# Single statistics passes between matmul groups, earlier residual sums, and one forward step ahead of an inverse step

## The chip, the cores and the metric

The kernel runs on one core of a Trainium2 chip. The metric is device time in microseconds (us); several executions give a median. A profile comes from one execution and shows each engine: TensorE (PE, its weight loads PEld), VectorE (DVE), ScalarE (ACT), GpSimd (POOL) and the queue that issues transfers (SP). Each engine works through its own list of instructions in order and waits on semaphores for the others.

## The reference

One sequence of 2048 tokens with 1024 features passes through four layers, A, B, A, B, with the same weights both times:

```
x = x + A(layernorm(x))      # A: 2-D real FFT over tokens and features, times a filter, inverse FFT
x = x + B(layernorm(x))      # B: mish(x @ w1 + b1) @ w2, w1 is 1024 x 3584, w2 is 3584 x 1024
```

and again. The layer norm subtracts the mean of a row of 1024 features and divides by the root of variance plus 1e-5. Mish is h * tanh(softplus(h)). Values are bf16, sums fp32.

## The kernel before, in words

The 2048 tokens are 16 tiles of 128, kept in SBUF as XS[0..15]. Every instruction is recorded in program order into a list for its engine, with the semaphore waits that its tiles ask for, so the order of calls in the source is the order on each engine.

**Layer A** does both transforms as matmuls in stages: a first stage (`s1`), then for each of eight groups g a forward step in two halves (`s2`, matmuls at L741, copied out at L776 by ScalarE or L778 by VectorE), a forward transform in two parts (`s3`, L786 to L789; ScalarE copies at L798, VectorE multiplies by the filter at L800 to L807), an inverse transform (`i1`, L842, copied by ScalarE at L858) and an inverse step (`i2`, L872 and L904). Results go to PSUM through pairs of banks taken in turn, four pairs in all. The order of these pieces is a string of numbers written out by hand in `order_A`; 221 stands for `s2` of group 2, half 1, and 400 for `i1` of group 0, part 0. In the first layer A the filter is also put together between steps (VectorE copies at L1043).

**Layer B** starts before the last stage of layer A is through. The first product with w1, `mm1`, takes 512 tokens (or a half of 256) and one group of 256 columns of w1: two runs of eight matmuls (L1220), each with its Mish on ScalarE (L1224), which frees the bank; three banks take turns. While the second halves of groups 1 to 3 run, ScalarE also makes the row sums of tiles 6 and 7 for their layer norm, in `stats_act`: one pass that copies and sums, one that squares and sums (L451, two per tile). VectorE turns the sums into mean and scale (L462 to L513), normalises (L522), and TensorE transposes the tiles (L1181, copied by VectorE at L1186) for the next `mm1`.

The larger part of layer B multiplies blocks by a scheme with seven products instead of eight. For w1 that is `quads`: in turn n of its loop the products (L1260) go to six banks, VectorE adds them up (L1265), and ScalarE applies Mish (L1270). Between the additions of two turns a hook, `after(n)`, puts in other work: statistics of tiles 8 to 11, their normalisation (`normal`), and the residual sums of tiles 12 to 15 (`residual`, L1498), which add layer A's result to XS. The last layer B has ten turns in this loop, the first has eight. In a turn the next product into a bank waits for the addition that reads that bank. After `quads` come the products with w2 (L1359, added at L1402 and L1410).

The lines that the change touches in `after(n)`, with `first` = 6 in the last layer and 4 in the first:

```
for j in {first + 1: (12, 13), first + 2: (14,), first + 3: (15,)}.get(n, ()):
    residual(j)
```

Of the kernel before, what the change touches and what calls it, by code (L numbers as in the profile page):

```python
# [5 lines left out]
ACT = mybir.ActivationFunctionType  # L6
# [174 lines left out]
class KB:  # L181
# [261 lines left out]
                writes=rr)  # L443
        self.op(self.dve, lambda e: e.reciprocal(r, a), writes=rr)

    def stats_act(self, j):
        act = self.act
        x, sums, rs, junk = self.XS[:, j, :], self.BN[:, j, 0:2], self.r_mv[j], self.junk
        rs.begin()
        for i, f in enumerate((ACT.Copy, ACT.Square)):  # L450
            self.op(act, lambda e, i=i, f=f: e.activation(junk.ap, x, f, accum_out=sums[:, i:i + 1]),  # L451
                    reads=[self.r_xs[j]], writes=[junk.res], parts=[rs])

# [551 lines left out]
    @staticmethod  # L1005
    def order_A():


        order = ("200 201 210 211 300 301 220 310 400 221 311 401 230 320 410 500 231 321 411 501 330 331 420 510 240 511 421 241 "
                 "250 251 340 341 520 350 430 260 521 431 440 261 351 441 530 531 360 361 270 450 451 271 540 541 550 551 460 370 "  # L1010
                 "461 371 560 561 470 471 570 571")
        return [tuple(map(int, w)) for w in order.split()]
# [144 lines left out]
    def layer_B(self, li, last):  # L1157
# [14 lines left out]
        def transposed(c, t, xn, eng=None, bank=None):  # L1172
            if bank is None:
                bank = 6 + nt[0] % 2
                nt[0] += 1
            xn.unread = False
            if t == 0:
                open_xt(c)
            fns = []
            for db in range(8):  # L1180
                fns.append(lambda e, db=db: e.transpose(PSb[:, bank, db * P:(db + 1) * P], xn.ap[:, db * P:(db + 1) * P],  # L1181
                                                        self.IDENT[:]))
            self.group(fns, reads=[xn.res, self.r_ident], writes=[self.r_bank[bank]])
            dst = XT[c].ap[:, :, t * P:(t + 1) * P]
            src = PSb[:, bank, :].rearrange("p (a b) -> p a b", b=P)
            fn = (lambda e: e.activation(dst, src, ACT.Copy)) if eng is act else (lambda e: e.tensor_copy(dst, src))  # L1186
            self.op(eng or dve, fn, reads=[self.r_bank[bank]], parts=[r_xt[c][t // 2]])
# [14 lines left out]
        def turn(n):  # L1202
            for _ in range(min(n, len(turning))):
                turning.pop(0)()

        def mm1(c, fg, half=None, mid=()):
            wb = self.w1_buf[fg]
            x = XT[c]
            tok = slice(0, 512) if half is None else slice(256 * half, 256 * half + 256)
            w = tok.stop - tok.start  # L1210
            for fl in range(2):
                if fl:
                    for f in mid:
                        f()
                ft = 2 * fg + fl
                bank = nh[0] % 3
                nh[0] += 1
                fns = []
                for db in range(8):
                    fns.append(lambda e, db=db, bank=bank, fl=fl: e.matmul(  # L1220
                        PS[:, bank, 0:w], wb.ap[:, db, fl * P:(fl + 1) * P], x.ap[:, db, tok], start=(db == 0), stop=(db == 7)))
                self.group(fns, reads=[wb.res] + (r_xt[c] if half is None else [r_xt[c][half]]), writes=[self.r_bank[bank]])
                at, ra = at_of(c, ft), r_at[c % 2][ft]
                self.op(act, lambda e, bank=bank, ft=ft, at=at: e.activation(at[:, tok], PS[:, bank, 0:w], ACT.Mish,  # L1224
                                                                      bias=self.B1[:, ft:ft + 1]),
                        reads=[self.r_bank[bank], self.r_b1], writes=[ra])
# [118 lines left out]
        def load_b(stages, n, k):  # L1345
            PB[n][k] = load_w2(stages[n][1], k, f"R{(2 * n + k + 1) % 4}")
# [20 lines left out]
        def products(p, s_off, stages, extra, loads=True):  # L1367
# [83 lines left out]
            for n, t in turn_of:  # L1451
                a, b, g, start = stages[n]
                bank = sets[g][t]
                if n or t:
                    tile_product(n, t, bank, ap[a], lambda k: part(a, k), start)
                after(b, t, bank)
                for f, k in sums.get((n, t), ()):
                    f(k)
                if t == 3 and n < 5 and loads:
                    for k in range(2):  # L1460
                        if stages is STD or (n, k) != (4, 0):
                            load_b(stages, n + 2, k)
                extra(n, t)
# [9 lines left out]
        def at_tiles(c):  # L1473
            r_at[c] = [None] * NF
            for k in range(2):
                off = self.ob["A"] + 14336 * (2 * k + c)
                AT[c][k] = b = self.alloc(f"AT{c}{k}", off, [NF // 2, 512])
                for i in range(NF // 2):
                    r = r_at[c][2 * i + k] = Res(f"AT{c}_{2 * i + k}")
                    r.inherit(b.res)  # L1480
                    self.live.append((off + i * 1024, off + i * 1024 + 1024, r))
# [15 lines left out]
        def residual(j):  # L1497
            self.op(dve, lambda e: e.tensor_tensor(self.XS[:, j, :], self.XS[:, j, :], YS[:, j - 4, :], ALU.add),  # L1498
                    reads=[r_ys[j // 4 - 1]], writes=[self.r_xs[j]])

        def turns(c, *ts):
            return [lambda t=t: transposed(c, t, xn[4 * c + t]) for t in ts]
# [50 lines left out]
            xn[j] = self.apply(j)  # L1553
        for fg in range(1, 4):
            mm1(0, fg, 1)
            if fg < 3:
                self.stats_act(5 + fg)
        if not last:
            mm1(0, 4)
        at_tiles(1)  # L1560
        B = {"B11": (XT[0].ap[:, 0:4, :], r_xt[0]), "B21": (XT[0].ap[:, 4:8, :], r_xt[0])}
        order = list(early)
        if last:
            block, corner, run = quads(list(range(4, 14)), order, B, [k * 1024 for k in (102, 140)])
            for n, bank in ((0, 3), (1, 4), (2, 5), (3, 0)):
                block(n, bank)
            corner(1, 4)
            turns(1, 0)[0]()
            corner(2, 5)
            turns(1, 1)[0]()  # L1570
            corner(3, 0)
        else:
            mm1(0, 5, mid=turns(1, 0, 1))
# [13 lines left out]
        def normal(j):  # L1587
            if j % 4 == 0:
                open_xt(j // 4)
            turned(j // 4, j % 4, self.apply(j))  # L1590
# [33 lines left out]
        def after(n):  # L1624
            again = {0: 7, 4: 8, 5: 9} if last else {0: 7}
            if n in again:
                self.fill_slot(order[again[n]], plain + again[n])
            if 1 <= n < 4:
                load_b(STD, n // 3, (n - 1) % 2)
            first = 6 if last else 4  # L1630
            if last:
                if n in (0, 2, 4, 5):
                    self.stats_act(8 + (0, 2, 4, 5).index(n))
                if n == 5:
                    self.xn_buf = self.xn_out + [self.alloc(f"XN{i}", self.ob["XN2"] + i * 2048, [self.D]) for i in range(2)]
                if n in (5, 7):
                    self.sums_to_mv(n + 3, 2)
                    self.scales(n + 3, 2)
            elif n < 4:
                self.stats_dve(8 + n)  # L1640
            elif n == 4:
                self.scales(8, 4)
            if n >= first:
                normal(8 + n - first)
                turn(4)
            for j in {first + 1: (12, 13), first + 2: (14,), first + 3: (15,)}.get(n, ()):
                residual(j)
        run(after, lead)
        self.junk = self.alloc("JUNK2", self.ob["JUNK2"], [self.D])
# [68 lines left out]
        order = [ws[n % 3] for n in range(14)]  # L1718
# [94 lines left out]
```

## Time and profile before

| | |
|---|---|
| median of 3 runs | 927.1 us (926.85 to 933.89) |
| profiled execution, span | 923.2 us |
| TensorE busy | 877.7 us, 95% |
| VectorE busy | 623.4 us, 68% |
| ScalarE busy | 435.0 us, 47% |
| GpSimd busy | 147.7 us, 16% |
| transfers | 175.98 MB, mean 191 GB/s |

The shares are means over stages. The page also gives the chain of work that ended last, followed back from the end, by engine and line. A list of waits gives, for each engine, which line waited for which line of another engine. A timeline gives start, duration, engine, line, operation and tiles; in brackets stands the idle time before an instruction and what ended it. Matmul ends are modelled, so a matmul's shown duration can run past the start of the next.

### The profile page before, as it was taken

Reading aid. Unit: us, or ns where it says so; the run is one execution under the profiler, and the core shown is the slowest. Engines: PE = TensorE matmul, PEld = TensorE weight load, DVE = VectorE, ACT = ScalarE, POOL = GpSimd, SP = SyncE. Lnnn points to the kernel's source line nnn. Section 1 sums busy time; section 2 is a strip of 40 time slices with the busy share of each in tenths; the row PEclk is TensorE's granted clock in tenths of the full one; section 3 lists DMA queues with packets and bytes.
Section 4 is the critical chain, followed back from the end, with each engine's and each line's share of the span. In section 5 each row is a group of like instructions: output and inputs, shape, how many; then the busy total and the mean of one; then the engine's idle time right before and its main releaser. Section 6 shows DMA issues by size and latency. Waiting matters only on the chain.

```text
span 923.2 us, 13610 instructions
## 1 busy us (share of the span) xinstructions
PE 877.7 (95%) x5503; PEld 471.1 (51%) x5503; DVE 623.4 (68%) x995; ACT 435.0 (47%) x645; POOL 147.7 (16%) x170
## 2 busy tenths in 40 slices
PE   0899889999999999999998998999999999999998
PEld 0677576444444444444456766754444444444443
DVE  7798468686889667568767765676747655554463
ACT  7898485456203485420018966757540025552000
POOL 0732004960004651010121200000000000000000
PEclk9999999999999999999999999999999999999999
DMA  9979861575786388364723786345166645732432
GB/s 279 284 249 287 219 194 67 210 266 139 262 281 239 131 317 298 121 233 143 281 92 114 221 217 161 137 175 184 23 197 189 204 148 180 269 121 86 173 129 102
DMA packets 153502, 175.98 MB, mean 191 GB/s; under 512 B 75000, under 2 KB 132568, under 8 KB 153320
## 3 DMA queue, kind: packets, MB, share of 16 engines
q1 hardware_dynamic: 140256, 130.32, 45.9%
q0 software_dynamic: 10032, 42.90, 12.5%
q10 hardware_dynamic: 3152, 1.90, 0.7%
q8 instruction: 43, 0.70, 0.3%
q14 instruction: 19, 0.16, 0.0%
HBM read 130.78 MB, written 40.89 MB: 186 GB/s over the span
## 4 chain that ended last, share of the span: by engine, by line
PE 88%; DVE 6%; ACT 3%; SPq 2%; DMA 1%; issue 0%; DVEq 0%
PE PS L1359 37%; PE PS L1260 30%; PE PS L1220 6%; PE PS L741 3%; PE PS L842 2%; PE PS L872 2%; SPq L251 2%; PE PS L1071 2%; PE PS L634 1%; PE PS L651 1%; ACT ARENA L640 1%; PE PS L1181 1%; PE PS L904 1%; PE PS L1060 1%; ACT ARENA L451 1%; PE PS L656 1%
## 5 line engine op out<-in xcount | busy, mean ns | idle before, releaser
L1359 PE MATMUL PS<-ARENA 128*128 128x512 bf16 x1568 | 340.1, 379 | 0.0
L1260 PE MATMUL PS<-ARENA 128*128 128x512 bf16 (+1 forms) x1288 | 280.4, 379 | 0.8 <-DVE ARENA L1265 0.8
L1359 PEld LDWEIGHTS PS<-ARENA 128*128 128x128 bf16 x1568 | 153.3, 98 | 184.5
L1265 DVE TENSOR_TENSOR ARENA<-PS,ARENA 128x512 f32<-128x512 f32 x230 | 157.1, 691 | 100.2 <-PE PS L1260 92.4
L1260 PEld LDWEIGHTS PS<-ARENA 128*128 128x128 bf16 x1288 | 125.3, 98 | 153.3 <-DVE ARENA L1265 3.6
L1270 ACT ACTIVATE ARENA<-ARENA,B 128x512 bf16<-128x512 f32 x138 | 98.8, 721 | 69.1 <-DVE ARENA L1265 63.8
L573 ACT ACTIVATE ARENA<-PS 128x512 f32<-128x512 f32 (+3 forms) x86 | 61.6, 726 | 110.6 <-PE PS L1260 92.5
L1153 POOL TENSOR_TENSOR ARENA<-ARENA 128x512 bf16<-128x512 bf16 x56 | 71.5, 1278 | 74.3 <-DVE ARENA L522 61.1
L451 ACT ACTIVATE ARENA<-XS 128x1024 bf16<-128x1024 bf16 x60 | 63.2, 1053 | 36.6 <-DVE XS L1410 33.0
L1220 PE MATMUL PS<-ARENA 128*128 128x256 bf16 (+1 forms) x528 | 73.4, 295 | 3.4 <-DVE ARENA L1186 1.9
L1384 DVE TENSOR_TENSOR ARENA<-ARENA 128x3584 bf16<-128x3584 bf16 x32 | 63.9, 2017 | 0.0
L1410 DVE TENSOR_TENSOR XS<-PS,ARENA 128x512 bf16<-128x512 f32 x52 | 35.7, 689 | 39.0 <-PE PS L1359 38.7
L1220 PEld LDWEIGHTS PS<-ARENA 128*128 128x128 bf16 x528 | 50.3, 98 | 22.3 <-DVE ARENA L1186 3.3
L1402 DVE TENSOR_TENSOR ARENA<-PS,ARENA 128x512 f32<-128x512 f32 x48 | 32.9, 688 | 28.0 <-PE PS L1359 27.6
L1224 ACT ACTIVATE ARENA<-PS,B 128x256 bf16<-128x256 f32 (+1 forms) x66 | 33.0, 515 | 29.0 <-PE PS L1220 28.8
L1270 ACT ACTIVATE ARENA<-PS,B 128x512 bf16<-128x512 f32 x46 | 31.5, 685 | 18.4 <-PE PS L1260 18.4
L1398 DVE TENSOR_TENSOR ARENA<-ARENA,XS 128x512 f32<-128x512 f32 x52 | 36.8, 731 | 0.5
L442 ACT ACTIVATE RS<-MV,EPS 128x1 f32<-128x1 f32 (+2 forms) x11 | 3.3, 296 | 71.5 <-DVE MV L564 70.1
L741 PE MATMUL PS<-FD,ARENA 128*128 128x256 bf16 (+1 forms) x256 | 31.4, 271 | 2.5 <-ACT ARENA L640 2.5
L842 PE MATMUL PS<-ARENA 128*128 128x256 bf16 x256 | 32.6, 273 | 1.0 <-DVE ARENA L807 0.6
L798 ACT ACTIVATE ARENA<-PS 128x1024 bf16<-128x1024 f32 x30 | 30.4, 1046 | 5.0 <-PE PS L789 5.0
L1235 DVE TENSOR_TENSOR ARENA<-ARENA 128x2048 f16<-128x2048 bf16 x16 | 25.3, 1583 | 9.0 <-PE PS L1220 8.7
(102 smaller groups left out, 811.4 us busy)
## 6 DMA issues: line engine op xcount, KB each, us to landing
ARENA<-in_B_w_dram SPq DMA_DIRECT2D x30, 896.0 KB, 6.7
ARENA<-w1s_scratch SPq DMA_DIRECT2D x28, 896.0 KB, 4.7
ARENA<-w2s_scratch SPq DMA_DIRECT2D x24, 896.0 KB, 6.6
w1s_scratch<-ARENA POOLq DMA_DIRECT2D x14, 896.0 KB, 4.6
ARENA<-in_B_w_dram SPq DMA_DIRECT2D x24, 512.0 KB, 4.3
u_scratch<-ARENA SPq DMA_DIRECT2D x14, 512.0 KB, 4.9
ARENA<-u_scratch SPq DMA_DIRECT2D x14, 512.0 KB, 6.0
w2s_scratch<-ARENA POOLq DMA_DIRECT2D x8, 896.0 KB, 4.1
```

What stands on the lines that cost most here:

```text
L451: self.op(act, lambda e, i=i, f=f: e.activation(junk.ap, x, f, accum_out=sums[:, i:i + 1]), reads=[self.r_xs[j]], writes=[junk.res], parts ...
L573: fn = (lambda e: e.activation(dst, src, ACT.Copy)) if scale is None else \
L741: fns.append(lambda e: e.matmul(dst, at(r), FD[:, t:t + n], start=start, stop=stop))
L842: fns.append(lambda e, c=c, part=part: e.matmul(ps[:, c * 256:(c + 1) * 256], yk.ap[:, part, c * P:(c + 1) * P], t[:, (128, 0)[part]:(384, ...
L1153: self.op(self.pool, lambda e, dst=A(dst), x=A(x), y=A(y), op=op: e.tensor_tensor(dst, x, y, op), reads=[b.res] + list(after), writes=[b.rs])
L1220: fns.append(lambda e, db=db, bank=bank, fl=fl: e.matmul(PS[:, bank, 0:w], wb.ap[:, db, fl * P:(fl + 1) * P], x.ap[:, db, tok], start=(db ...
L1260: self.group([lambda e, db=db: e.matmul(PS[:, bank, :], A[:, db, :], mov[:, db, :], start=(start and db == 0), stop=(db == 3), skip_group_ ...
L1265: self.op(dve, lambda e: e.tensor_tensor(dst.ap, PS[:, bank, :], x.ap, ALU.add), reads=[self.r_bank[bank], x.res], writes=[dst.res])
L1270: self.op(act, lambda e: e.activation(at, src, ACT.Mish, bias=self.B1[:, ft:ft + 1]), reads=[res, self.r_b1], writes=[ra])
L1359: self.group([lambda e, i=i, k=k, b=PB[n][k].ap: e.matmul(PS[:, bank, :], ap[:, i, t * P:(t + 1) * P], b[:, i - 7 * k, :], start=(start an ...
L1384: self.op(dve, lambda e: e.tensor_tensor(ap[dst][:, f, :], ap[x][:, f, :], ap[y][:, f, :], op), reads=part(x, k) + part(y, k), writes=part ...
L1398: self.op(dve, lambda e: e.tensor_tensor(a[t], a[t], x, ALU.add), reads=[rx], writes=[r[t]])
```

## The change

It has three parts, all of them moves; no arithmetic is added or removed.

1. `stats_act` can do one of its two passes. The four passes over tiles 6 and 7, which followed groups 1 and 2 in pairs, now follow groups 1, 2, 3 and one later piece of work one at a time. The later piece is group 4 in the first layer B and a corner product of `quads` in the last. The aim is that Mish of a group doesn't stand behind two passes.
2. In the last layer B's `quads` loop the residual sums of tiles 12 and 13 move from turn 7 to turns 1 and 3; those of 14 and 15 stay in turns 8 and 9. In the first layer B the turns stay what they were (5, 6, 7).
3. In `order_A` the second half of group 2's forward step (221) comes ahead of the first inverse transform (400), in both layers A.

```
-    def stats_act(self, j):
+    def stats_act(self, j, passes=(0, 1)):
...
-        rs.begin()
-        for i, f in enumerate((ACT.Copy, ACT.Square)):
+        if passes[0] == 0:
+            rs.begin()
+        for i in passes:
+            f = (ACT.Copy, ACT.Square)[i]
...
-        order = ("200 201 210 211 300 301 220 310 400 221 311 401 230 ...
+        order = ("200 201 210 211 300 301 220 310 221 400 311 401 230 ...
...
         for fg in range(1, 4):
             mm1(0, fg, 1)
-            if fg < 3:
-                self.stats_act(5 + fg)
+            self.stats_act(6 + fg // 3, ((fg - 1) % 2,))
         if not last:
             mm1(0, 4)
+            self.stats_act(7, (1,))
...
             corner(1, 4)
+            self.stats_act(7, (1,))
             turns(1, 0)[0]()
...
-            for j in {first + 1: (12, 13), first + 2: (14,), first + 3: (15,)}.get(n, ()):
+            late = {1: (12,), 3: (13,), 8: (14,), 9: (15,)} if last else {5: (12, 13), 6: (14,), 7: (15,)}
+            for j in late.get(n, ()):
                 residual(j)
```

More of the change, by code (lines that the diff above doesn't have):

```diff
@@ L1006, in order_A @@
     def order_A():
-        order = ("200 201 210 211 300 301 220 310 400 221 311 401 230 320 410 500 231 321 411 501 330 331 420 510 240 511 421 241 "
+        order = ("200 201 210 211 300 301 220 310 221 400 311 401 230 320 410 500 231 321 411 501 330 331 420 510 240 511 421 241 "
                  "250 251 340 341 520 350 430 260 521 431 440 261 351 441 530 531 360 361 270 450 451 271 540 541 550 551 460 370 "
```

## Prediction

> **What bounds the kernel now.** I read, in this order: the page's shares and the chain that ended last, TensorE's list of waits, the timelines of TensorE and ScalarE around each named wait, and the chain inside those stretches. The page first:
>
> ```profile
> PE 877.7 (95%) x5503; PEld 471.1 (51%) x5503; DVE 623.4 (68%) x995; ACT 435.0 (47%) x645; POOL 147.7 (16%) x170
> PE 88%; DVE 6%; ACT 3%; SPq 2%; DMA 1%; issue 0%; DVEq 0%
> ```
>
> TensorE carries 88% of the chain, at the full granted clock in all 40 slices. No edit removes a matmul. The change can only gain idle time of TensorE, so I list who makes it wait (total us, times, longest us):
>
> ```profile
> PE PS L1220 <- ACT ARENA L1224: 1.4, 3, 0.6
> PE PS L1260 <- DVE ARENA L1265: 0.8, 1, 0.8
> PE PS L786 <- DVE ARENA L778: 0.8, 1, 0.8
> PE PS L842 <- DVE ARENA L807: 0.6, 1, 0.6
> ```
>
> Four waits lie where the edits are: L1220 (first product of layer B behind Mish), L1260 behind L1265 (the quadrant loop behind a VectorE addition), and L786 and L842 in layer A. Now their places. First TensorE, then ScalarE, early in the first layer B (start, duration, instructions, idle before in brackets):
>
> ```profile
> 134.39 4.53 PE L1220 MATMUL PS<-ARENA 128*128 128x256 bf16 x40
> 139.53 2.77 PE L1220 MATMUL PS<-ARENA 128*128 128x256 bf16 x16 [0.62 <-ACT ARENA L1224]
> 142.47 3.63 PE L1220 MATMUL PS<-ARENA 128*128 128x512 bf16 x16 [0.17 <-ACT ARENA L1224]
> ```
> ```profile
> 136.79 1.06 ACT L451 ACTIVATE ARENA<-XS 128x1024 bf16<-128x1024 bf16 x1
> 137.97 1.06 ACT L451 ACTIVATE ARENA<-XS 128x1024 bf16<-128x1024 bf16 x1
> 139.02 0.82 ACT L1224 ACTIVATE ARENA<-PS,B 128x256 bf16<-128x256 f32 x2
> 139.74 1.05 ACT L451 ACTIVATE ARENA<-XS 128x1024 bf16<-128x1024 bf16 x1
> 141.97 1.40 ACT L1224 ACTIVATE ARENA<-PS,B 128x256 bf16<-128x256 f32 x3
> ```
>
> Both passes of tile 6 stand in ScalarE's queue ahead of group 2's Mish, which had its matmuls since 137; the product cycles through three banks, so TensorE stops at 139.53 until that Mish frees one. The same with tile 7 at 142.47.
>
> The quadrant loop of the second layer B, from its chain:
>
> ```profile
> 654.42 0.69 DVE ARENA L1265
> 657.08 0.54 DVE FD L522
> 657.62 1.20 DVE XS L1498 x2
> 658.82 0.61 DVE ARENA L1265
> 659.48 4.49 PE PS L1260 x20
> ```
>
> Between two additions VectorE does scales, one normalisation (L522) and the two residual sums of tiles 12 and 13 (1.20 us); TensorE restarts only after the addition behind them. And the second layer A:
>
> ```profile
> 497.53 0.38 PE L789 MATMUL PS<-ARENA 128*128 128x512 bf16 x1
> 498.55 1.05 PE L842 MATMUL PS<-ARENA 128*128 128x256 bf16 x8 [0.64 <-DVE ARENA L807]
> 499.43 1.04 PE L741 MATMUL PS<-FD,ARENA 128*128 128x256 bf16 x8
> ```
>
> The inverse step (L842) waits for VectorE's filtered product, while the forward step behind it (L741) needs nothing late.
>
> The bracketed idle is short. A 512-column matmul is shown as 0.38 us, but 384 of them took 82.90 us on the chain, 0.216 each. So I count the gap from start plus 0.216 (8 of 256 columns: 0.87).
>
> **What the Trainium skill says.** "Perfetto Trace Analysis", section Per-engine timelines, calls ScalarE and VectorE strict FIFO and TensorE's ends estimates. The trace agrees on both: the ready Mish stood behind two passes for 2 us, and shown ends overrun the next start. "ScalarE: Activation LUTs", section What ACT_TABLE_LOAD costs, prices an ACTIVATE with immediate operands at 186 ns + 0.833 ns per element, 1039 ns for 1024; the trace shows 1038 to 1058, plus an accumulator read of 187 ns, and pass to pass 1.18 us. It also prices a switch of function set; between Mish and statistics at 136 to 145 us no table load is seen, so finer interleaving adds none.
>
> **The change part by part.**
>
> *Statistics of tiles 6 and 7, first layer B.* The four passes stay; one now follows each of groups 1 to 4. I replay ScalarE: group 1's Mish ends 136.80; pass 6a to 137.97; group 2's two Mish to 138.8; pass 6b to 140.0; group 3's first Mish to 140.45, its second to 140.85; pass 7a to 142.0. TensorE: its last group before the stop ends at 134.39 + 5 x 0.87 = 138.74; it then wants the bank of group 2's first Mish, now done at 138.4. It goes on; group 4's first half (512 columns, 1.73 us) runs 139.6 to 141.3 and its second needs the Mish of 140.45. No stop is left. Gaps gained: 139.53 - 138.74 = 0.79, and 142.47 - (139.53 + 0.87 + 1.73) = 0.34. Sum 1.13 us.
>
> *The moved wait.* Pass 7b now stands behind group 4's second Mish and ends near 145.1 instead of 142.06. VectorE's small operations on these sums (L462) wait for it; queued behind are the scales, the normalisation of tiles 6 and 7, and then their transposes on TensorE. In the trace L462 runs at 147.79, after the copies of transposed tiles 4 and 5. With TensorE 1.13 earlier that becomes 146.65: 1.5 us of slack. No cost.
>
> *The same, second layer B.* One gap: 586.83 - (581.68 + 5 x 0.87) = 0.80 us. Here pass 7b follows the Mish of the first corner. Replayed: four bank copies end at 591.1, that Mish at 592.0, pass 7b at 593.2; VectorE comes to L462 at 594.59 - 0.80 = 593.8. Slack 0.6 us. The first blocks start 0.8 us earlier, at 586.87, on weights whose loads were issued at 579.36, 581.88 and soon after with 3.5 to 4.6 us to landing; the last block, at 589.5, needs the one that lands near 587.5. No cost.
>
> *Residual sums of 12 and 13.* Only the last layer's schedule moves. The 1.20 us between the additions goes. VectorE's addition then runs from about 657.6 to 658.2. TensorE's preceding matmul ends at 659.48 - 0.78 - 0.38 + 0.22 = 658.54, so it no longer stops: 0.94 us gained. At the new places one residual each (0.60 us) goes in front of an addition that waits for TensorE anyway: in the loop's early turns VectorE works 3.38 us and idles 1.03 (613.55 to 626.79). 0.60 fits into 1.03, and GpSimd is idle from 609.8 to 669, so the 1.58 us per sum of the first layer B's four does not apply. No cost.
>
> *Forward step ahead of inverse step, second layer A.* TensorE stops from 497.75 to 498.55, 0.80 us. The forward step (0.87) fills it; the inverse step runs 498.62 to 499.49, the next forward step (0.86) to 500.35. Then the second inverse step wants a product that VectorE ends at 500.07 + 0.42, so it starts near 500.55, where 501.17 was: 0.62 us kept. ScalarE gets the forward copy before the inverse copy but was idle 0.51 us there, and runs about 0.6 earlier afterwards.
>
> *The same, first layer A.* The chain from 42.04 to 58.41 lies on VectorE without a break (filter copies, products), and TensorE's stop of 0.76 at 58.46 ends with it. The moved step is copied by ScalarE; VectorE's order is unchanged. No gain; at most the 0.2 us gap at 46.73 moves.
>
> *Sum.* 1.13 + 0.80 + 0.94 + 0.62 = 3.49 us. Each gap is followed by TensorE at full rate (82.90 and 81.58 us pieces of the chain), and what starts later is released by TensorE, so it moves along. 927.1 - 3.5 = 923.6 us.
>
> **The rivals.** *A: part is lost.* The 0.62 of layer A returns as waits on VectorE, or the shortened loops run into weight transfers. For it: in layer A VectorE and ScalarE stay nearly full (16.80 and 20.46 of 23 us). Against: TensorE's list has no wait for weights after the start. If layer A and the second layer B's first gap are lost: 927.1 - 1.13 - 0.94 = 925.0.
>
> *B: slower.* The late pass 7b becomes the last wait of the normalisation, and the early residuals delay their additions. If replay is off by a whole pass plus the slack, tiles 6 and 7 come 1.2 us later in each layer; their transposes had about 0.65 us (150.50 to 151.18), so 0.55 twice, and 0.3 twice for the residuals. With nothing gained: 927.1 + 1.1 + 0.6 = 928.8. Against it: VectorE reaches those sums only after the transposes, which the trace shows as a 2.58 us idle before 146.59.
>
> *C: more.* The first layer A also loses its 0.76 stop at 58.46, and the late stops in the second layer A shrink: 927.1 - 3.5 - 0.8 - 0.3 = 922.5. Against it: VectorE's unbroken chain.
>
> **How the numbers follow.** Forecast 0.68, A 0.18, B 0.06, C 0.08. The predicted time is the forecast's, 923.6. The range runs from C, less a little for the spread between runs (926.85 to 927.1 among two of three), to somewhat above A: 922.1 to 926.3; B and an outlier like 933.89 lie outside. One per cent is 9.3 us, over twice the sum of all gaps, so same has 0.96; 0.02 on each side is left for what no view shows.
>
> **What would show it.** In the profile after: in both layers B no wait of L1220 on L1224 inside the second halves, and single passes of L451 between pairs of Mish; L462 still preceded by the copies of transposed tiles, not by idle time on ScalarE; the wait of L1260 on L1265 gone; L1498 singly in the early turns with shorter idle there; in the second layer A the wait of L842 down to some 0.2 us, in the first an unchanged 0.76 at L786. The span should be 919.7. It is wrong if L462 waits for L451, if a wait on a weight transfer appears, or if the gaps close but reopen before the layer ends.

## The result and the profile after

| | before | after |
|---|---|---|
| median of 22 runs each | 927.6 us (926.15 to 933.89) | 924.94 us (922.73 to 927.64) |
| span of the profiled execution | 923.2 us | 922.2 us |
| TensorE busy | 877.7 us | 877.0 us |

The ratio is 0.9964, 95% interval 0.9955 to 0.9974: 927.6 x 0.0036 = 3.3 us less, between 2.4 and 4.2. The forecast was 3.5 less. (The ratio isn't the quotient of the two medians: that is 0.9971, or 2.7 us less. The means give 0.9966, or 3.2 us.)

Code lines after `stats_act` stand two further down in the changed kernel: L1220 is L1222 there, L1260 is L1262, L786 is L788, L842 is L844 and so on.

First the page's shares and its chain, after the change:

```profile
PE 877.0 (95%) x5503; PEld 471.3 (51%) x5503; DVE 623.5 (68%) x995; ACT 434.7 (47%) x645; POOL 148.7 (16%) x170
PE 88%; DVE 5%; SPq 4%; DMA 2%; ACT 2%; issue 1%; ACTq 0%; DVEq 0%
```

The work is the same to the instruction. On the chain VectorE and ScalarE lost a per cent each; the queue that issues transfers gained two and the transfers one. The first is the change. The second is where this one execution lost much of the gain again. TensorE's list of waits shows both (total us, times, longest):

```profile
PE PS L636 <- DMA ARENA<-in_A_x_dram: 4.6, 2, 3.9
...
PE PS L788 <- DVE ARENA L780: 1.1, 1, 1.1
PE PS L636 <- DMA ARENA<-ARENA: 0.9, 1, 0.9
...
PE PS L1073 <- DMA ARENA<-u_scratch: 0.4, 1, 0.4
```

Three of the four waits that the prediction named are no longer in the list: L1222 on L1226, L1262 on L1267, L844 on L809. The fourth, L788 on L780 in the first layer A, is there with 1.1 instead of 0.8 us. And there are waits on transfers: the load of x stood in the list before with 2.7 us, the other two are new in it.

Early in the first layer B, TensorE and then ScalarE (start, duration, instructions; the accumulator reads are left out):

```profile
135.44 10.58 PE L1222 MATMUL PS<-ARENA 128*128 128x256 bf16 x72
145.86 1.06 PE L1183 MATMUL PS<-IDENT,ARENA 128*128 128x128 bf16 x16
```
```profile
137.83 1.06 ACT L453 ACTIVATE ARENA<-XS 128x1024 bf16<-128x1024 bf16 x1
...
138.89 0.82 ACT L1226 ACTIVATE ARENA<-PS,B 128x256 bf16<-128x256 f32 x2
139.60 1.05 ACT L453 ACTIVATE ARENA<-XS 128x1024 bf16<-128x1024 bf16 x1
...
140.64 0.83 ACT L1226 ACTIVATE ARENA<-PS,B 128x256 bf16<-128x256 f32 x2
141.35 1.06 ACT L453 ACTIVATE ARENA<-XS 128x1024 bf16<-128x1024 bf16 x1
...
144.92 1.05 ACT L453 ACTIVATE ARENA<-XS 128x1024 bf16<-128x1024 bf16 x1
```

Where TensorE had three pieces with idle time between them, it has one of 72 matmuls. Passes (L453) and pairs of Mish (L1226) take turns. The second layer B shows the same, before and after:

```profile
586.83 1.05 PE L1220 MATMUL PS<-ARENA 128*128 128x256 bf16 x8 [0.61 <-ACT ARENA L1224]
```
```profile
582.44 5.40 PE L1222 MATMUL PS<-ARENA 128*128 128x256 bf16 x48
```

In the first layer B the last pass ends at 145.97 and its read at about 146.06. The wait that was moved there is on VectorE:

```profile
146.50 1.29 DVE L1188 COPY ARENA<-PS 128x1024 bf16<-128x1024 bf16 x2 [1.45 <-PE PS L1183]
147.71 0.16 DVE L464 TENSOR_SCALAR MV<-BN 128x4 f32<-128x4 f32 x1
```

L464, which needs that pass, follows the copy of transposed tiles with no bracket, so no idle time: the pass was done 1.6 us before. In the second layer B the read of the pass ends at 593.93 and L464 runs at 594.57, again without idle time: 0.6 us.

The quadrant loop of the last layer B, on VectorE, before and then after, at the first of the two moved sums:

```profile
622.38 3.38 DVE L1265 TENSOR_TENSOR ARENA<-PS,ARENA 128x512 f32<-128x512 f32 x5 [1.03 <-PE PS L1260]
```
```profile
621.23 0.68 DVE L1500 TENSOR_TENSOR XS<-XS,ARENA 128x1024 bf16<-128x1024 bf16 x1
622.35 3.38 DVE L1267 TENSOR_TENSOR ARENA<-PS,ARENA 128x512 f32<-128x512 f32 x5 [0.44 <-PE PS L1262]
```

The addition behind the sum still waits 0.44 us for TensorE, where it waited 1.03: the sum fills idle time. TensorE runs 244 matmuls without a break from 609.78 to 662.99. And the second layer A on TensorE:

```profile
498.58 1.04 PE L743 MATMUL PS<-FD,ARENA 128*128 128x256 bf16 x8
499.46 1.04 PE L844 MATMUL PS<-ARENA 128*128 128x256 bf16 x8
...
501.38 1.05 PE L844 MATMUL PS<-ARENA 128*128 128x256 bf16 x8
```

The forward step (L743) runs in what was the stop, and the inverse step (L844) follows it at once.

To say what each edit is worth I measured the stretches between the same two TensorE instructions, start to start, in both profiles (A0, B0 the first layers, A1, B1 the second; us):

| stretch | before | after | difference | forecast |
|---|---|---|---|---|
| span's start to A0's first stage | 23.97 | 25.04 | +1.07 | 0 |
| A0 to the transposes of tiles 0, 1 in B0 | 93.87 | 93.85 | -0.02 | 0 |
| B0, transposes 2, 3 to transposes 4, 5 (statistics) | 16.48 | 15.35 | -1.13 | -1.13 |
| B0, transposes 4, 5 to A1 | 335.15 | 336.07 | +0.92 | 0 |
| A1, first `s2` to first `i2` (forward step) | 13.65 | 13.04 | -0.61 | -0.62 |
| A1, first `i2` to last stage | 53.56 | 54.10 | +0.54 | 0 |
| B1, transposes 2, 3 to 6, 7 (statistics) | 22.36 | 21.56 | -0.80 | -0.80 |
| B1, start of `quads` to first product with w2 (sums) | 53.99 | 53.04 | -0.95 | -0.94 |
| B1, first product with w2 to the end | 259.40 | 259.38 | -0.02 | 0 |

The stretches not listed are equal. The four gains sum to 3.49 us. The three losses sum to 2.53, and nearly all of it is waits on transfers: the load of x at the start, the transfer that A1's first stage waits for (0.9 in the list, 0.69 of the 0.92 in its row), and the read of u_scratch (0.4 in the list, 0.54 in its row). The other 0.23 lies inside the first layer B: a weight load that waits for VectorE's L1404 at 281.8 us costs TensorE 0.16, and one that waits for a load of w1s_scratch at 357.3 costs less than 0.1. That is why these two spans differ by 1.0 only, and why the span is 922.2 where the prediction said 919.7, while the medians of 22 runs differ by 2.7. The profile before was a lucky one in this: of the 13 profiles of this document it has the earliest first stage (23.97 us, 24.09 to 25.04 in the others) and is the only one without a wait for u_scratch.

### The profile page after: what moved, and what is told of

It reads as the page before. It is cut to its first block, busy times and chain, and to the rows that moved or that the text cites. A ratio compares the mean times of both kernels' runs of the same rounds, so it can differ in the third digit from the quotient of the medians.

```text
span 922.2 us, 13611 instructions
## 1 busy us (share of the span) xinstructions
PE 877.0 (95%) x5503; PEld 471.3 (51%) x5503; DVE 623.5 (68%) x995; ACT 434.7 (47%) x645; POOL 148.7 (16%) x170
## 4 chain that ended last, share of the span: by engine, by line
PE 88%; DVE 5%; SPq 4%; DMA 2%; ACT 2%; issue 1%; ACTq 0%; DVEq 0%
PE PS L1361 37%; PE PS L1262 30%; PE PS L1222 7%; SPq L251 4%; PE PS L743 2%; PE PS L844 2%; PE PS L874 2%; PE PS L1073 2%; PE PS L1183 1%; DMA ARENA<-in_A_w_i_dram 1%; PE PS L906 1%; ACT ARENA L642 1%; PE PS L788 1%; DVE ARENA L1188 1%; DMA ARENA<-u_scratch 1%
## 5 line engine op out<-in xcount | busy, mean ns | idle before, releaser
L1262 PE MATMUL PS<-ARENA 128*128 128x512 bf16 (+1 forms) x1288 | 280.3, 379 | 0.0
L1267 DVE TENSOR_TENSOR ARENA<-PS,ARENA 128x512 f32<-128x512 f32 x230 | 157.1, 690 | 99.4 <-PE PS L1262 91.6
L1262 PEld LDWEIGHTS PS<-ARENA 128*128 128x128 bf16 x1288 | 125.5, 98 | 152.2 <-DVE ARENA L1267 2.1
L453 ACT ACTIVATE ARENA<-XS 128x1024 bf16<-128x1024 bf16 x60 | 63.2, 1053 | 36.3 <-DVE XS L1412 33.0
L1222 PE MATMUL PS<-ARENA 128*128 128x256 bf16 (+1 forms) x528 | 72.9, 295 | 2.0 <-DVE ARENA L1188 1.9
L1222 PEld LDWEIGHTS PS<-ARENA 128*128 128x128 bf16 x528 | 50.5, 98 | 20.1 <-DVE ARENA L1188 3.3
L1404 DVE TENSOR_TENSOR ARENA<-PS,ARENA 128x512 f32<-128x512 f32 x48 | 32.9, 688 | 28.1 <-PE PS L1361 27.7
L1226 ACT ACTIVATE ARENA<-PS,B 128x256 bf16<-128x256 f32 (+1 forms) x66 | 33.2, 515 | 28.0 <-PE PS L1222 27.8
L743 PE MATMUL PS<-FD,ARENA 128*128 128x256 bf16 (+1 forms) x256 | 31.4, 271 | 2.5 <-ACT ARENA L642 2.5
L844 PE MATMUL PS<-ARENA 128*128 128x256 bf16 x256 | 32.6, 273 | 0.3
```

What stands on the lines that cost most here:

```text
L743: fns.append(lambda e: e.matmul(dst, at(r), FD[:, t:t + n], start=start, stop=stop))
L844: fns.append(lambda e, c=c, part=part: e.matmul(ps[:, c * 256:(c + 1) * 256], yk.ap[:, part, c * P:(c + 1) * P], t[:, (128, 0)[part]:(384, ...
L1222: fns.append(lambda e, db=db, bank=bank, fl=fl: e.matmul(PS[:, bank, 0:w], wb.ap[:, db, fl * P:(fl + 1) * P], x.ap[:, db, tok], start=(db ...
L1262: self.group([lambda e, db=db: e.matmul(PS[:, bank, :], A[:, db, :], mov[:, db, :], start=(start and db == 0), stop=(db == 3), skip_group_ ...
L1267: self.op(dve, lambda e: e.tensor_tensor(dst.ap, PS[:, bank, :], x.ap, ALU.add), reads=[self.r_bank[bank], x.res], writes=[dst.res])
```

## The experiments

Ratios are against the kernel before, run on the same chip. Stretches are those of the table, from one profile of each kernel.

**Part 1 alone: the statistics passes.** The kernel before with the first part of the diff (`stats_act` by single passes, one after each group), nothing else.

> Only the single statistics passes, both layers B. My account: both stops of L1220 on L1224 go, 1.13 us in the first layer B and 0.80 us in the second, so the stretch from the transposes of tiles 2 and 3 to those of tiles 4 and 5 shortens by 1.1 us and the one to the first block by 0.8; the stop of L1260 at the residual sums (0.78 shown) and that of L842 (0.64 shown) stay. Time 1.9 us below the kernel before, ratio 0.998. Rival (ScalarE is the bound there, stops only move): the stretch to the transposes keeps its length, ratio 1.000.

Ratio 0.9982 (0.9969 to 0.9995); median 925.94 us. The two stretches were 15.35 and 21.57 us, as in the changed kernel, while the loop's 54.00 and A1's 13.65 stayed as before. The part works alone, by the forecast amount.

**Part 2 alone: the residual sums.** The kernel before with

```
-            for j in {first + 1: (12, 13), first + 2: (14,), first + 3: (15,)}.get(n, ()):
+            late = {1: (12,), 3: (13,), 8: (14,), 9: (15,)} if last else {5: (12, 13), 6: (14,), 7: (15,)}
+            for j in late.get(n, ()):
```

> Only the residual sums of tiles 12 and 13 at turns 1 and 3. My account: the stop of L1260 behind L1265 goes, 0.94 us, nothing opens at turns 1 and 3; the four stops of the other two parts stay. Ratio 0.999. Rival (the early sums delay their additions): new idle of L1260 on L1265 near 623 or 633 us of up to 0.3 each, ratio 1.000.

The loop took 53.04 us, the forecast 0.95 less than before; the other stretches with an edit stayed. VectorE's timeline shows the same thing as in the changed kernel, the sum of one tile in the idle time in front of an addition:

```profile
630.65 0.68 DVE L1498 TENSOR_TENSOR XS<-XS,ARENA 128x1024 bf16<-128x1024 bf16 x1
631.77 3.38 DVE L1265 TENSOR_TENSOR ARENA<-PS,ARENA 128x512 f32<-128x512 f32 x5 [0.44 <-PE PS L1260]
```

The ratio, however, was 1.0007 (0.999 to 1.0024), median 928.68 us. The expected gain of 0.1% lies at the edge of this interval, so the total time neither shows it nor excludes it. The profiled execution waited 3.1 us for the transfer at A1's entrance, at a place that comes before anything that this kernel changes; there its granted clock fell to 0.50 for 6.83 us, and A1's first stage took 12.32 us instead of 9.91.

**Part 3 alone: the forward step.** The kernel before with `310 221 400` in place of `310 400 221` in the order.

> Only the forward step 221 ahead of 400. My account: second layer A 0.62 us shorter between the start of s2 and the third i1, first layer A unchanged (chain on VectorE, stop at L786 stays 0.76 to 1.1 us). Ratio 0.9993. Rival: the gain returns later in layer A, so the stretch from the first s2 matmul to the last i1 of the second layer A keeps its length, ratio 1.000.

A1's stretch was 13.04 us, 0.61 less; the stop of L786 in the first layer A stayed, with 1.1 us instead of 0.76, as in the changed kernel. Ratio 1.0000 (0.9989 to 1.0012): the expected 0.9993 is inside, so is no change. Again the stretch shows the effect and the time can't.

**Is it the bank? More banks instead of moved passes.** The kernel before, with its passes still in pairs, but the second halves of groups 1 to 3 go through five banks instead of three:

```
-        def mm1(c, fg, half=None, mid=()):
+        def mm1(c, fg, half=None, mid=(), spare=None):
...
-                bank = nh[0] % 3
+                bank = spare[2 * (fg - 1) + fl] if spare else nh[0] % 3
...
-            mm1(0, fg, 1)
+            mm1(0, fg, 1, spare=(1, 2, 0, 6, 7, 1))
...
+        nh[0] = 1 if last else 2
```

> The kernel before with its statistics passes in pairs, but the second halves of groups 1 to 3 of the first product take five PSUM banks (0, 1, 2, 6, 7) where three took turns. If the stops come from a bank that waits for a Mish behind two passes, they go without moving a pass: 1.1 us and 0.8 us, ratio 0.998, same stretches as with single passes. Rival (the stops are ScalarE's total work, or the order of passes itself matters): the stops stay or appear one group later, ratio 1.000.

In the first layer B the stretch fell to 15.35 us, exactly as with the moved passes, and TensorE ran 72 matmuls in one piece:

```profile
136.34 10.58 PE L1220 MATMUL PS<-ARENA 128*128 128x256 bf16 x72
```

So the stop was the wait for a bank that a late Mish held; a pass on ScalarE costs TensorE nothing by itself. But the ratio was 1.0008 (0.9994 to 1.0022), because the stops reappeared in TensorE's list at the loop behind:

```profile
PE PS L1260 <- ACT ARENA L1224: 0.8, 1, 0.8
...
PE PS L1260 <- ACT ARENA L573: 0.6, 1, 0.6
```

In the first layer B the first quadrant product finds its bank held by the last Mish, and the stretch from the transposes of tiles 6, 7 to the loop grew from 19.31 to 20.25 us. In the second, ScalarE's copies for the first blocks stand behind the pair of passes, and the stretch from the first block to the transposes of 6, 7 grew from 11.40 to 12.14. That returns 0.94 + 0.74 of the 1.9 us. The 0.74 is the wait of the passes at a new place: ScalarE's queue still has them in pairs. The 0.94 belongs to this edit's choice of banks. Its last line sets the turn of the three banks to 2, where the kernel before comes to 1; 20 runs of matmuls later the last Mish holds bank 0, the bank of the first quadrant product, and not bank 2. Another choice of five banks might keep that part; it wasn't run.

**How much room is in an early turn? One sum back.** The changed kernel with tile 13's sum in turn 7 again, tile 12's in turn 1:

```
-            late = {1: (12,), 3: (13,), 8: (14,), 9: (15,)} if last else ...
+            late = {1: (12,), 7: (13,), 8: (14,), 9: (15,)} if last else ...
```

> The changed kernel with the residual sum of tile 13 back at turn 7 (tile 12 stays at turn 1). One sum costs VectorE 0.60 us there, so the stop of L1260 behind L1265 should come back by 0.94 - 0.60 = 0.34 us counted from start to start (0.2 shown). Rival (any residual sum at turn 7 costs the full stop, or none does): 0.94 or 0.

The loop took 53.39 us, 0.35 more than in the changed kernel. TensorE's list again has the wait, small:

```profile
PE PS L1262 <- DVE ARENA L1267: 0.2, 1, 0.2
```

**All four sums in turn 7.** As above with `{7: (12, 13, 14, 15)}`.

> The changed kernel with the residual sums of tiles 12, 13, 14 and 15 all at turn 7. VectorE has 4 x 0.60 us there instead of 2: stop 0.94 + 1.20 = 2.1 us counted from start to start, and nothing at turns 8 and 9. Rival (a stop that doesn't follow VectorE's time): 0.9 us as in the kernel before.

The loop took 55.20 us, 2.16 more than in the changed kernel:

```profile
PE PS L1262 <- DVE ARENA L1267: 2.0, 1, 2.0
```

With one, two and four sums in turn 7 the loop is 0.35, 53.99 - 53.04 = 0.95 and 2.16 us longer than with none: each sum beyond the first costs its full 0.60, and the first 0.35, since 0.25 of it is free. (Each time the list shows 0.15 to 0.17 us less than the stretch, for the reason that the prediction gave: the modelled ends cover part of a gap.) Each of these two kernels ran once, 925.81 and 925.09 us; the one with the longer loop was the shorter, so a single time tells nothing here.

**Overdrawing the slack of the moved wait.** The changed kernel, but in the first layer B both passes of tile 7 come behind the whole first group of the next tokens:

```
-            self.stats_act(6 + fg // 3, ((fg - 1) % 2,))
+            if fg < 3 or last:
+                self.stats_act(6 + fg // 3, ((fg - 1) % 2,))
...
-            self.stats_act(7, (1,))
...
+            self.stats_act(7)
```

The last line stands behind `mm1(0, 5)`.

> The changed kernel, first layer B only: both passes of tile 7 behind the Mish of group 5 instead of behind groups 3 and 4. They would end at 149.4 + 2.4 = 151.8, so VectorE's first operation on the sums waits for ScalarE by some 4 us and the transposes of tile 6 on TensorE come about 3.4 us later than in the changed kernel; the second layer B is unchanged. That is the price when the slack of 1.5 us is overdrawn. Rival (the sums have slack enough anyway, the transposes are not the next thing TensorE needs): under 0.5 us.

VectorE now waits for the pass, and TensorE for VectorE's normalisation:

```profile
151.85 0.17 DVE L464 TENSOR_SCALAR MV<-BN 128x4 f32<-128x4 f32 x1 [3.82 <-ACT ARENA L453]
```
```profile
154.64 1.08 PE L1183 MATMUL PS<-IDENT,ARENA 128*128 128x128 bf16 x16 [3.14 <-DVE ARENA L524]
```

From the transposes of tiles 4, 5 to those of 6, 7 it took 8.55 us instead of 5.24, 3.31 more. From there to the loop another 1.45 was lost (20.76 instead of 19.31), which I hadn't expected. No engine kept TensorE waiting there. It ran without a break, in 20.01 us where the changed kernel takes 18.58 for the same piece. From 155.95 to 159.36 us, behind the stop of 3.14, its granted clock was 0.50 of full speed (the third number from the end of the second line):

```profile
155.55 20.01 PE L1222 MATMUL PS<-ARENA 128*128 128x256 bf16 x102
```
```profile
155.95:159.36 3.41, 3.41 (x18) 2.44 (x17) 3.34 (x4) 0.95 (x2) 3.25 (x3) 0.50 0.00 0
```

One run took 928.85 us. The 3.31 us are the prediction's slower rival made real; in the changed kernel the slack holds.

**The stop left in the first layer A: a filter copy on GpSimd.** In the changed kernel, one group's filter copies (L1045) go from VectorE to GpSimd, which is nearly idle there:

```
-                             self.JT, self.r_jt, dve)
+                             self.JT, self.r_jt, pool if g == 3 else dve)
```

> The changed kernel with the filter copies of group 3 in the first layer A (two copies, 1.3 us) on GpSimd instead of VectorE. If VectorE's unbroken chain is what keeps the first layer A from gaining, the stop of L786 (1.14 us shown) closes by most of 1.1 us and the stretch from the first L778 copy to that matmul shortens by about as much: ratio to the kernel before 0.995. Rival (another bound right behind, ScalarE or GpSimd's queue): the stop stays or moves to a wait on GpSimd, ratio 0.996 or above.

Wrong. The stop of L788 on L780 went, but a larger one came. VectorE, GpSimd and TensorE in this kernel:

```profile
48.19 2.98 DVE L807 TENSOR_TENSOR ARENA<-ARENA 128x512 bf16<-128x512 bf16 x1
```
```profile
48.87 2.79 POOL L1045 COPY ARENA<-ARENA 128x1024 bf16<-128x1024 bf16 x2
```
```profile
52.00 1.89 PE L844 MATMUL PS<-ARENA 128*128 128x256 bf16 x8 [2.63 <-DVE ARENA L809]
```

VectorE's product L807, 0.43 us elsewhere in this profile, lasted until half a microsecond before GpSimd's two copies were through. VectorE gave away copies that take it 1.36 us and lost 2.5. Behind TensorE's stop the granted clock was 0.50 from 51.42 to 54.83 us, which adds to the loss. The stretch from VectorE's first copy L780 to the `s2` of group 4 took 22.72 instead of 19.80 us. The ratio was 0.9981 (0.9968 to 0.9995) where the changed kernel has 0.9964. The Trainium skill's "GPSIMD Engine Reference", section Specifications, says that GpSimd's SBUF interfaces are shared with VectorE and contend with its instructions that have two SBUF inputs; L807 is one, and the trace agrees. The timing isn't clean, though: L807 starts 0.68 us before the copies are shown to start, and the shown spans of GpSimd are rough. Better evidence, from the profile before, stands in the last section.

**The same stop, by another order.** In the changed kernel, for the first layer A alone, `230 320 410 500 231 321` becomes `230 231 320 410 500 321`.

> The changed kernel, and in the first layer A alone 231 (second half of group 3's forward step, copied by VectorE) ahead of 320, so that VectorE makes its copy before the products of group 2 and not after the first of them. If the stop of L786 comes from the place of that copy at the end of VectorE's unbroken chain, the copy is done some 2 us earlier and the stop goes (1.14 us shown); the pair of PSUM banks that 231 holds longer may give up to 0.5 us back at 321. First s2 matmul to the first transposes of layer B shorter by 0.6 to 1.1 us; ratio to the kernel before 0.9955. Rival (VectorE's sum of work is the bound, the order doesn't matter): the stop reappears at a later product, stretch unchanged, ratio 0.9964.

The stop didn't go, it moved to an earlier product (L788, step 321) and grew:

```profile
58.63 0.39 PE L788 MATMUL PS<-ARENA 128*128 128x512 bf16 x1 [1.69 <-DVE ARENA L780]
```

VectorE did come to the copy of 231 earlier, by about the forecast 2 us: in the kernel with both orders, further down, it starts 13.14 us after VectorE's first copy L780, in the changed kernel 15.04. But that product needs the pair of banks that 231 holds until it is copied, and TensorE, with 231 moved ahead, now asks for this pair as early as step 321. With both orders, 321 starts 14.42 us after the first copy instead of 12.51, and VectorE later waits 0.66 us for ScalarE's copy of a delayed product. The stretch from the first copy L780 to the `s2` of group 4 took 21.53 us instead of 19.80. Of these 1.7 us, 1.06 is a VectorE wait at 46.76 us, shortly after TensorE waited 0.9 us for a load of the filter; with both orders there is no such wait, and 0.71 us is lost. Ratio 0.9973 (0.9962 to 0.9985). My expectation failed. So did the rival, which had the stop at a later product and the stretch unchanged. VectorE's sum of work isn't all that sets the end of this stretch; which step waits for which pair of banks counts too.

**The last 0.2 us of the second layer A.** In the changed kernel, for the second layer A alone, `311 401 230 320` becomes `311 230 401 320`: one more forward step goes ahead of an inverse one.

> The changed kernel, and in the second layer A alone 230 ahead of 401. The rest of 0.19 us that the second inverse transform still waits for VectorE should go: first s2 matmul to first i2 matmul 12.85 us instead of 13.04 (13.65 before). Rival (the later copy of that inverse transform now makes i2 wait for ScalarE): 13.04 or more.

A1's stretch was 12.84 us, 0.20 less than in the changed kernel. The prediction had put the remaining gap there down to VectorE's product. In the changed kernel's profile that product (L809) ends at 501.33 us and the inverse step starts at 501.38, so it is. Ratio 0.9972 (0.996 to 0.9983).

**Both orders together.**

> The changed kernel with both orders: 231 ahead of 320 in the first layer A, 230 ahead of 401 in the second. Sum of the two: 0.8 to 1.3 us below the changed kernel, ratio to the kernel before 0.9953. Rival: no gain over the changed kernel, 0.9964.

A1's stretch 12.83 us; in the first layer A the stop remained as

```profile
56.45 0.39 PE L788 MATMUL PS<-ARENA 128*128 128x512 bf16 x1 [1.23 <-DVE ARENA L780]
```

and the stretch there took 0.71 us more than in the changed kernel. Ratio 0.9963 (0.9944 to 0.9982), no better than 0.9964. None of these kernels can be told from the changed one as faster. The second order alone gains 0.2 us in its stretch, which no time here could show.

## Why the prediction was right

*Statistics, first and second layer B.* 1.13 and 0.80 us forecast, 1.13 and 0.80 measured, also with this part alone (15.35 and 21.57 us). More banks removed both stops at their places without moving a pass, so the mechanism is shown, not only the size.

*The moved wait.* Forecast at no cost with 1.5 and 0.6 us of slack. The pass was done 1.6 and 0.6 us before VectorE came to it. Where the slack was overdrawn, TensorE paid 3.31 us at the very place that the slower rival had named.

*Residual sums.* 0.94 forecast, 0.95 measured; idle in front of the next addition 0.44 instead of 1.03, which is the 0.60 that the working put there.

*Forward step, second layer A.* 0.62 forecast, 0.61 measured. The remaining gap was the wait for VectorE's product, and the other order filled it.

*First layer A.* No gain forecast, none found: 93.87 and 93.85 us. The stop at L788 is 1.14 instead of 0.76, but the stretch around it, from VectorE's first copy L780 to group 4's forward step, is 19.80 instead of 19.90. VectorE's unbroken chain was the reason given, and it holds: from VectorE's first copy L780 to its second takes 15.04 to 15.22 us in all ten profiles in which VectorE's work there is the same, while TensorE's stop behind the second is 0.76 to 0.78 in the four with the old order and 1.09 to 1.36 in the six with the new one. TensorE only comes to the stop earlier. That the stop would stay at 0.76 was wrong. Two attempts to get round the chain, by GpSimd and by order, both failed, each for a reason of its own.

*The sum, and the rivals.* 3.5 us forecast, 3.3 measured (2.4 to 4.2), or 2.7 by the medians. The time forecast was 923.6 us, and 924.94 came; 0.5 of the difference is that the starting point of 927.1 was a median of three runs. Taken alone, 924.94 fits rival A's 925.0 better than the forecast. It is the stretches that decide for the forecast: rival A had layer A's gain and the second layer B's first gap lost, and both are there. Rival B (slower) and rival C (the first layer A also gains) are excluded by the profile. Of rival A, the losses it named, gains given back in layer A or waits for weights in the shortened loops, are not in the profile, except for less than 0.1 us at one weight load in the first layer B, and in the profile before TensorE's weight loads waited for the same transfer too, 0.3 us. But waits on other transfers are there, most of the 2.53 us in that one execution; the prediction put them at nothing.

What stays open is whether the change makes these waits any longer on average. At A1's entrance the wait was absent in the profile before and 0.9 us after; but it was absent with part 1 alone, 3.1 with part 2 alone, and between 0.4 and 2.4 in the nine other kernels. It is longest in a kernel that changes nothing ahead of that place, and there is one profile of each, so these profiles can't separate an effect from chance. Also, the ratios of the three parts alone add up to a gain of 0.18 - 0.07 + 0.00 = 0.11%, less than the 0.36% of all together. Their intervals, half-widths 0.13, 0.17 and 0.12, combine to about 0.25, so this is just compatible with parts that add up, and no more than that.

The granted clock, which is on record for each run, explains some of it. It differs between runs of one kernel: in 100 runs of the kernel before, from three of the comparisons, the median is 927.15 us at a mean clock of 1.000 (52 runs), 928.36 at 0.998 (33) and 929.84 at 0.996 (8). Among the runs at 1.000 alone, the mean gain over the kernel before is 1.7 us for part 1 (11 runs), 1.0 for part 2 (7) and 0.7 for part 3 (10), against 1.93, 0.94 and 0.62 forecast. Together that is 3.4. This choice of runs was made after the fact, and each gain has a standard error of about 0.5 us, so it agrees with the forecast and doesn't prove it.

## What to carry to other kernels

Price a stop of a pipelined engine from start to start of the instructions around it, at the spacing measured where nothing waits; here that gave gaps to 0.02 us, where the shown idle time was up to 0.17 short. Where side work shares an engine with work that frees a buffer, put it in pieces no longer than the slack between two uses of that buffer, or into idle time that the engine has anyway, and then check what waits for the last piece. Edits worth a tenth of a per cent are judged by the stretch that they touch: the total time of part 2 and of part 3 alone couldn't show gains that their stretches show plainly. And before a longer stretch is put down to a wait, the granted clock inside it has to be read.

## What the runs showed of the hardware

A copy on GpSimd held up a VectorE instruction with two SBUF inputs for nearly its whole length: 2.98 us instead of 0.43, beside copies of 2.79. This was not a slowdown by some share but close to a standstill. The profile before shows which instructions suffer. Beside GpSimd's products L1153, VectorE's L1498 (both inputs in SBUF) takes 1.64 us in four cases, and 0.68 in the twenty others; L1235, also with both in SBUF, takes a median of 2.06 instead of 1.22. L1265, which has one input in PSUM, takes 0.69 in 37 cases beside GpSimd and in 193 without.

In eight of the 13 profiles the granted clock falls to 0.50 for 3.41 us, in three cases for 6.83 us, each time at or close behind stops of TensorE. Behind the stop of 2.63 us above, eight matmuls of 256 columns took 1.89 us where 1.04 is usual. Most often it happens early in a layer B, where each profile has stops of about 0.74, 0.87 and 0.93 us within some 4 us. From the transposes of tiles 0, 1 to those of 2, 3 it takes 11.62 us at the full clock; this is so in 21 of 26 cases (13 profiles, two layers). In four it took 13.27 or 13.28 with 3.41 us at half the clock, and in one, in the profile of part 1 alone, 14.30 with 6.83. No edit touches that stretch. Why the same stops are followed by half the clock in some executions and not in others isn't shown. Nor is it shown that the change makes this rarer: 10 of its 22 runs have a mean clock of 0.998 or less, and 31 of 59 of the kernel before.
